# Two PSUM banks per eviction: any two banks read by one strided view, against neighbouring banks or one instruction per bank, with a new order table

## The chip, the cores and the metric

The kernel runs on one core of a Trainium2 chip. Time is device time in microseconds (us) of one execution. TensorE is called PE, VectorE DVE, ScalarE ACT, GpSimd POOL, and SP is the queue that issues DMAs. PE accumulates into PSUM, which has 8 banks of 512 float32 columns in each of the 128 partitions; here the whole of it is one tile, `ps`, and bank `u` is its columns from `512 * u`.

## The reference, cut to what matters

```python
# q, k, v: (4, 8, 768, 48); beta: (4, 8, 768)
k_n = k / (norm(k) + 1e-6)
for t in range(768):                      # a delta rule: one 48x48 state per head
    y[t] = q[t] @ state
    v_old = state^T @ k_n[t]
    state += beta[t] * outer(k_n[t], v[t] - v_old)
x = y.reshape(4, 768, 384)
h = relu(x @ w_in)                        # 384 -> 1024
u, v = h[..., :512], h[..., 512:]
v_n = (v - mean(v)) / sqrt(var(v) + 1e-6)
v_s = einsum('ts,bsd->btd', w_spatial, v_n) + b_spatial[None, :, None]
out = (u * v_s) @ w_out                   # 512 -> 384
```

## The kernel before, in words

The delta rule is done in chunks of 64 positions. The 4 x 8 heads and the 12 chunks give 24 steps (`s`), of which steps 0 to 11 are one chain through the state `st_` (tile `s`) and steps 12 to 23 another. Four steps make a group (`g`). `prep(g)` multiplies the keys of each step with themselves on PE (`kk`, 16 matmuls into two PSUM banks), copies the two banks to SBUF in one instruction (`ev`, the COPY `xt<-ps` or `wspl<-ps` of L339), and inverts small triangular blocks in a long chain of tiny operations: of groups 0 and 1 on DVE (`lanes16`, L571, L574, L576, working in a PSUM bank of its own), of groups 2 to 5 on POOL (`lanes`, L556, L561). `widen` then doubles the blocks with PE, ACT, DVE and POOL (`pi` of L641; `move`, four COPYs `xt<-xt`; `zero`, four MEMSETs of L638).

`step(s)` is the recurrence: `a_` on PE (keys times state), a subtraction on DVE (L720, `bn<-bn,ps`), `qs` and `b_` on PE, `w` on ACT (L748), `c_` on PE, the state on DVE (L761, `s<-s,ps`), `pu` on PE and the output copy `ye` on ACT (L778, `xs<-ps`). `kqt(s)` multiplies keys and queries into two banks (`kq`) and masks them on DVE (L695, `pt<-ps,mpos`). So three kinds of instruction read a pair of banks: `ev`, the mask and `ye`, 24 of each.

Every two steps yield 128 positions of two batches for the MLP: `mlp_v`, `mlp_u` (from `xh`, `xl` and `win_h`, `win_l`: each factor is split into two fp32r parts), and after each chain `gate`: the spatial product (`wsph`, `wspl` with `vf`, 792 matmuls in all) and the output product (`wout_h`, `wout_l` with `g`). The weights are split on ACT, DVE and POOL in the beginning (`win_h<-ut` of L386, `win_l` of L387). All matmuls stand under L463, since one helper issues them, and many plain copies under L339.

What runs when is written out: `P.add` records about 2,400 operations with their dependences, and `ORDER`, a table of two-letter numbers, lists them in the order in which they are issued; `PICK` says for an operation that two engines can do which one does it. Each engine works its own part of that list off in order. `Qq` in the table is a filler: one 128x256 matmul of `mpos` into a free bank (28 are built). Banks come from the pool `pm`, which is a queue: a request takes the bank that has been free longest, and an operation that wants two takes the first two, whichever they are. Banks 0 and 1 (`pc`) belong to the recurrence. An instruction that reads a pair does it through one access pattern:

```python
def banks(hs):
    a, b = sorted(h.unit for h in hs)
    v = ps[:, a * 512 : a * 512 + 256]
    return bass.AP(v.tensor, v.offset, [list(v.ap[0]), [(b - a) * 512, 2], [1, 256]])
```

The framework finds from the access patterns which instruction must wait for which, and sets semaphores. In the program as built, 38 of the reads of two banks have one to four other banks between the two (28 on ACT, 10 on DVE).

Of the kernel before, what the change touches and what calls it, by code (L numbers as in the profile page):

```python
# [17 lines left out]
GP = 4  # L18
# [24 lines left out]
    "2k4f2)2*2+2-2.5i3p3q2/2:2<5n3Z3x3c3yQq2%4N5j0[1F1f133r3s3u4g5o1G1#1T3v4h5p5l1H141s4m4O2>2?2@2[2]2^2_2{2|2}2~2,303132"
    "33342=35363738393t3A3B4Q3C4S3D4R3E4TQq4iQq4U5m5r5s5u5t1t1g4j1U1u5v4k1h4V3#3&3!3(5q8x3%3$4l3)4W5w5xQq4Z1y1z4a4d3w4c4b"
    "8l3*5y5z1vQq5!5#5$1!5%5&3F3G5(5*423+433-44454X6o1$3H3I5+5-5.5/5:5;5<5=5>6p3.463<3=3/5L4n5M1%473:3>5?5@5[5]5^5_5{5|5}"
    "5K4Y4p5N4o3?5O5P4q3;1&1(1)6g5~5,60616263643@4r4A4s4t4w4x3[1*1+8m5V8n6h4B4C4z3z5Q4u5R4D5S4(4e4&4$1-4*8o6566676n3]6i5W"
    "4E4)4y4#4%FR6j6k486l68696A6B6C6D6E6F6G5T5)6%4v5U3^498p6q6r6m8q3_4F5X6&6(4H1<5a5b4G4+6s6H6I6J6K6L6M6N6O5Z5YQq6t6u1.1/"
    "6/6x6v1:1;6y8u4!8r6!6#6z6P4-6Q6R6:1=1>6S6T6U6V6$5c5d7i6w1?6.3{1@4.6)6*4/6+5C8s8t7j4:4;8v4<5DQq6;7k8w7l6W1[6X6Y1]8!8y"
    "7(6-6Z1^6a6b6c6<6=4>4?6>3|8z7m8#6?7n1_6_6|3}6d6e7p7o6f7:8$1{4@4[4]5E6@6]4^6^8%7)5455565F7*8&575G7+6{736~716,72706}8("
    "8)8*8+8-8.8/5H587q59417-1|5I7.5J5B748:8<8=8>8?8@8[8]8^8_8{6[9n9o7s7r7t9.7u7v5A9p9q9r7w1}4=1~9s7/8|758}Qq8~8,7x7;9/7y"  # L50
    "767z7=7%7$7#7|7<4_90209192937>9:1,7!A;21777S4|4{7?7@7C7D7[7_7E947]7{229t9v95967~83817}9798997^9w239u789;7F3~9<9=A<7G"
    "7HA=9A24259B7T9x9y4}26797A7B7I9z9!A>3,4~9#808485827&86279)7,9C4,A?Ap9D879E7U7V7W9&9$7X285053292A7K9(9F9%9?9G9>9H9IQq"
    "2BA@7Z7Y8c7a7b7c9]887d898d8e9@8f7e9^2DB89[8A7f9_9{8B9J9K2C2E7J7h9|8U9L8;7LA[40512F7g9M9N9O9}8C9,A0B98D9*9+A19~A{8V8E"
    "8WAAA8A2A39-A]2GA^9P2H9Q9RA_BA2I8FA6B48G8HBB2J7M8IA}8JBCA|BDA~Qq8g8X9S9TQq7N9U8K9VBF9WQqA7A9ArA5B5BEA,7OAs8YBG8h8M7P"
    "8j8ZAq8iB2B3At8LB0Av2K9X9Y9Z9a9b9c9dBHB1BIBKBJAwBL8bAuAx7QFFFIBM8aFGABFHBRB6AyBNGPQqFJAC8N8O528PFKBO9e9f9g9h9i9j9kAz"
    "A$8QGQFOFLA4BVBQBU9lGHBPIUGYBXBY8kBTB7BWQqADAEAJAKALAMANAZAFAGAHFMGi8RA!A#A%AOAIFNAPAQAR8SA&ASATAUFPAaAbAcFQAdAeAhAi"
    "GIGJGjGKGbGcGkFVFTFSFUFWGLGMGO9mGNAjAkAlHGGdGeAmHHGRFXQqFZQqFYBZFaFbFcGfGSIIGXA(GZBSA-A)HIHJGVAgGgAfAnGWAoFdBaFeFfBb"
    "FgFiGhFjFkFlFmFnFoFpGTBxAVHKAWGUByHOBcGlHdHPGnGmGoAXFqFrFsFtFu7RGpA.HL8TA*BzBhBiBdGqFvGrHNB!BeBfBjB#GsBkBlHeHQGvILGw"
    "FwHMFxBgGtBmHkFyBnHRBoBpFzF!F#F$BqA/GxGaGyGzB(HSB)B$HTHfHgHUHhBrBsHXBtHYB*G$G!GuHZHaG#G%BuB%B&HiA+B+HlHVHWB-HnJTF%F&"
# [12 lines left out]
    "E)L)E8L-L.L(L+L<L/LlL:L;E*MbEtE+McMdMsMeMfK3MpMqE/E:E;L9LAMgE<E=E>E?E@E[MtMhE]MuMvMwMiMxL=H~MjMyE^E_LBK=K>LCH,G}E-I0"
    "K?MzM!LHK@K[LDLILJLKK^LLLMLEK_K{K|E.L>G~E{LNK4K5E|K}LFM*M-M&M)M(EuK~M+M$M%E}M.LOM/K]K,G,LGL0E~L{L|MBL}MCL?MDL@L[M@L]"
    "L^L~L,M:M;M0L1L2M<L_M1M3M2MEM=M>MFM[MGM]M^NEM_MJM4M?M{M|M5L3L4M#M}M~L5M6M,N0M7L6M8N1L7M9MKE,F0MLNFN6N7N8MMNGNHNIF7F1"
    "F2F8F9FAMNF3MOFBF4N2N3N4NMFCNNNONPN9NQNRNSNTNUL8NVNWNXNcNdNeNfNgNhNiNjNYNZO>O]F5NaNbNkNlNmN+FDMHK6N-NJNnO^NoNpNqNrN."
    "N/N:NAN;N<N=N>N?N@N[N]N^NKMQN_MAN{N|N}N~O?N,O0O1O2O3O4O5O6OSOTNBO7O8O9OAOBMPOUNsOVOWOXOYOZOaObOcOdOiOKOjOkOlOmOCOnOL"
    "OoOpOqOrOsOtOeO<N5O|OuOvOwO@NCO_O=OxO}O{N!N#ODN$NtOMN%OENuN&ONNvNwOFNxOON(OGOPF6FEO[NyNLOfOgOhO~O,P0P1P2P3P4P5P6P7P8"
    "P9PAPBPCN)N*OQNzOROyOzOHPEO!O)PFO*PGPHPIPJPKPLO+PMPDO-PNPkPlPmPOO#O.PPPnPoPQPRPpPSPTPqO/O:PrPsPtO$PuPUO%PvP!PcP#PdPV"
    "PePfPgP$P%PwPxMIOIPyOJO&O(O;PzP&Q4Q5P(Q6Q7PWPXPYPZP)P*P+P-P.P/P:P;P<P=Q8Q9QAQBQCQDPhQEQFQKQLQMQNP|QOQPQQQGQRQSP}QTQU"
    "PiNDQHQIPaPjPbQVP>P?P~P,P@P[P]Q0P^QWQXQJQYQZP_Q1QaQbQcQdQeQiQfQjQkQlQ2P{Q3QgQhQmQnQoQp"  # L80
)
PICK = (
    "11101010011110100110100000000000000000000001110011000011001100000000000000000000001100010000000000000000000000100000"
    "00000000000011000000000100000001011101000010100011000101000000000100000000001100010000001101000010000111101001000001"
    "0110011011010000110001000000"
# [3 lines left out]
class Op:  # L89
    __slots__ = ("i", "fn", "alt", "pr", "deps", "out", "acq", "rel", "give", "kind", "kb", "rate", "port", "n", "t")  # L90
# [13 lines left out]

class Plan:
# [7 lines left out]
    def add(self, eng, dur, fn, rd=(), wr=(), pr=0.0, acq=(), rel=(), give=(), port=False, kb=0, kind="", rate=190.0):  # L113
        o = Op()
        o.i, o.fn, o.pr, o.acq, o.rel, o.give, o.kind, o.kb, o.rate = len(self.ops), fn, pr, acq, rel, give, kind, kb, rate
# [30 lines left out]
    def greedy(self):  # L146
# [3 lines left out]
        refs = {}  # L150
        for o in self.ops:
# [3 lines left out]
            if not o.deps:  # L155
                ready.append(o)
        while ready:
            can = [o for o in ready if all(units[p] >= sum(q == p for q, _ in o.acq) for p, _ in o.acq)]
# [4 lines left out]
            for p, _ in o.acq:  # L163
                units[p] -= 1
            for p, h in o.rel:
                refs[h] -= 1
                units[p] += refs[h] == 0
            for p, _ in o.give:
                units[p] += 1
# [7 lines left out]
    def emit(self):  # L177

        units = {p: list(u) for p, u in self.pools.items()}
        for o in self.ops:  # L180
# [3 lines left out]
        for o, e in list(self.listed() if ORDER else self.greedy()):  # L184
            if o is None:
                if units["pm"]:
# [873 lines left out]
```

## Time and profile before

| | |
|---|---|
| median of 3 runs | 511.7 us (511.24 to 514.7) |
| profiled execution | 514.14 us, of which its span (first to last instruction) is 512.4 us |
| mean granted TensorE clock | 0.893 of full speed |
| PE busy | 444.0 us (87%) |
| DVE, ACT, POOL busy | 248.9, 248.9, 223.6 us |

The page gives the busy time of each engine, the span in 40 slices, and the chain of work that ended last, followed back from the end. A row of a group of instructions ends in the idle time of the engine just before them and what released it. A row of the timeline starts with its start and its length in us and ends, where the engine had been idle, in brackets with that idle time and the releaser. Windows give the busy time of each engine within a stretch and the clock granted to PE, 1.00 being 2.4 GHz and 0.50 being 1.2 GHz.

### The profile page before, as it was taken

How to read it: one execution, taken by the hardware profiler on the slowest of the kernel's cores; microseconds unless marked ns; L12 is line 12 of the kernel's file. 1: busy time of each engine (PE TensorE's matmuls, PEld its weight loads, DVE VectorE, ACT ScalarE, POOL GpSimd, SP SyncE). 2: the span in 40 equal slices, each digit the busy share in tenths (PEclk: the TensorE clock that was granted, in tenths of full speed). 3: DMA queues.
4: the chain of work that ended last, by engine and by line, in shares of the span. 5: the costliest groups of instructions: out<-in, count | busy, mean ns of one | idle time of the engine just before them, and what ended most of it. 6: DMA issues, size and time to landing. Idle time of an engine off the chain costs nothing.

```text
span 512.4 us, 21714 instructions
## 1 busy us (share of the span) xinstructions
PE 444.0 (87%) x9728; PEld 392.5 (77%) x9728; DVE 248.9 (49%) x543; ACT 248.9 (49%) x577; POOL 223.6 (44%) x370
## 2 busy tenths in 40 slices
PE   4547955788897998779999989999999999999997
PEld 3436743667675687567799779998898889999996
DVE  3686834742575674774652813624454123333222
ACT  1576743435486687667624622426534375323211
POOL 3024440698448980248982686480212411414000
PEclk9655556695799999998999989999999999999999
DMA  8700332024232326753204305010144000000112
GB/s 279 269 3 20 92 99 65 35 62 151 75 114 82 108 80 207 218 155 120 74 4 147 95 23 160 23 36 3 32 131 118 10 18 17 17 2 0 63 51 74
DMA packets 26109, 42.65 MB, mean 83 GB/s; under 512 B 4512, under 2 KB 14880, under 8 KB 26016
## 3 DMA queue, kind: packets, MB, share of 16 engines
q1 hardware_dynamic: 26016, 41.27, 25.5%
q8 instruction: 76, 1.25, 1.0%
q14 instruction: 17, 0.14, 0.1%
HBM read 35.36 MB, written 4.72 MB: 78 GB/s over the span
## 4 chain that ended last, share of the span: by engine, by line
PE 76%; ACT 8%; DMA 6%; DVE 5%; issue 3%; SPq 1%; ACTq 0%; DVEq 0%
PE ps L463 76%; ACT xt L339 3%; DMA bn<-in_bun 2%; DVE prod L571 1%; DVE ps L574 1%; DMA vf<-in_w_in 1%; ACT xs L778 1%; DMA ke<-in_k_t 1%; SPq L354 1%; DMA xs<-xs 1%; ACT pi L641 1%; DVE pt L695 1%; ACT w L748 1%; ACT wspl L339 0%; ACT xh L799 0%
## 5 line engine op out<-in xcount | busy, mean ns | idle before, releaser
L463 PE MATMUL ps<-wsph,vf 128*128 128x256 f32 x528 | 108.1, 286 | 1.1 <-ACT xs L778 1.1
L463 PEld LDWEIGHTS ps<-wsph,vf 128*128 128x128 f32 x528 | 86.9, 191 | 2.6 <-ACT xs L778 1.6
L561 POOL TENSOR_TENSOR wl<-wl,prod 128x60 f32<-128x60 f32 (+7 forms) x120 | 73.6, 614 | 9.3
L463 PE MATMUL ps<-wspl,vf 128*128 128x256 f32 x264 | 74.6, 282 | 0.0
L556 POOL TENSOR_TENSOR prod<-wl,la 128x60 f32<-128x60 f32 (+7 forms) x120 | 67.6, 563 | 9.3
L917 DVE TENSOR_TENSOR gt<-ps,bbc 128x512 f32<-128x512 f32 x24 | 16.6, 691 | 76.2 <-PE ps L463 64.5
L463 PEld LDWEIGHTS ps<-wspl,vf 128*128 128x128 f32 x264 | 50.4, 191 | 0.3
L463 PE MATMUL ps<-wout_h,g 128*128 128x384 f32 x128 | 35.7, 347 | 2.5 <-ACT xs L778 2.5
L339 ACT COPY xt<-ps 128x256 f32<-128x256 f32 (+1 forms) x35 | 16.5, 474 | 39.3 <-PE ps L463 39.2
L695 DVE TENSOR_TENSOR pt<-ps,mpos 128x512 f32<-128x512 f32 x24 | 16.5, 686 | 36.6 <-PE ps L463 30.6
L680 POOL TENSOR_TENSOR bn<-bn,nn 128x384 f32<-128x384 f32 x12 | 10.6, 887 | 49.1 <-DVE nn L548 24.5
L463 PE MATMUL ps<-mpos 128*128 128x256 f32 x56 | 25.7, 575 | 7.2 <-POOL mpos L378 3.0
L463 PE MATMUL ps<-ke 64*64 64x64 f32 (+2 forms) x768 | 22.0, 268 | 11.3 <-issue 4.7
L463 PEld LDWEIGHTS ps<-ke 64*64 64x64 f32 (+1 forms) x768 | 17.9, 167 | 16.1 <-issue 7.5
L339 ACT COPY xt<-xt 32x128 f32<-32x128 f32 (+1 forms) x82 | 28.7, 350 | 1.7
L463 PEld LDWEIGHTS ps<-wout_h,g 128*128 128x128 f32 x128 | 23.7, 193 | 2.9 <-ACT xs L778 2.6
L748 ACT COPY w<-ps 128x384 f32<-128x384 f32 x24 | 11.5, 478 | 28.3 <-PE ps L463 28.2
L463 PE MATMUL ps<-pt,w 64*48 64x64 f32 x768 | 18.6, 242 | 7.3 <-ACT w L748 6.0
L882 ACT ACTIVATE ut<-ps 128x256 f32<-128x256 f32 x48 | 17.3, 380 | 14.7 <-PE ps L463 14.7
L463 PE MATMUL ps<-bn 64*64 64x64 f32 (+2 forms) x896 | 20.3, 242 | 4.6 <-ACT wspl L339 2.6
L922 ACT CAST xt<-gt 128x512 fp32r<-128x512 f32 x8 | 5.0, 620 | 38.7 <-DVE gt L920 28.7
L463 PEld LDWEIGHTS ps<-pt,w 64*48 64x48 f32 x768 | 14.9, 138 | 11.1 <-ACT w L748 7.2
(209 smaller groups left out, 1085.8 us busy)
## 6 DMA issues: line engine op xcount, KB each, us to landing
bn<-in_bun SPq DMA_DIRECT2D x46, 256.0 KB, 3.5
bn<-in_bun SPq DMA_DIRECT2D x48, 192.0 KB, 3.7
ke<-in_k_t SPq DMA_DIRECT2D x22, 256.0 KB, 3.4
out<-ob SPq DMA_DIRECT2D x24, 192.0 KB, 2.0
vf<-in_w_in SPq DMA_DIRECT2D x6, 512.0 KB, 6.7
g<-in_w_sp SPq DMA_DIRECT2D x3, 768.0 KB, 6.4
g<-in_w_out SPq DMA_DIRECT2D x4, 384.0 KB, 3.6
xs<-xs SPq DMA_DIRECT2D x66, 16.0 KB, 2.6
```

What stands on the lines that cost most here:

```text
L339: (nc.scalar.copy if e == "ACT" else ENG[e].tensor_copy)(out=out_, in_=in_)
L354: return P.add("SP", 0.39 if k.get("kb") else 0.57, lambda: nc.sync.dma_start(out=out_() if callable(out_) else out_, in_=in_() if callabl ...
L463: nc.tensor.matmul(o, l, r, start=start, stop=stop)
L556: P.add("POOL", cost, lambda: nc.gpsimd.tensor_tensor(out=pt if j else dst, in0=w3[:, :n, j : j + 1].broadcast_to([128, n, m]), in1=la3[:, ...
L561: P.add("POOL", cost, lambda: nc.gpsimd.tensor_tensor(out=dst, in0=dst, in1=pt, op=ALU.add), rd=["prod"], wr=[kw], pr=p0 + 2)
L571: P.add("DVE", cost, lambda: nc.vector.tensor_tensor(out=pt(), in0=w4()[:, :, :n, j : j + 1].broadcast_to([128, 2, n, m]), in1=lj.unsqueez ...
L574: P.add("DVE", cost, lambda: nc.vector.tensor_tensor(out=dst(), in0=dst(), in1=pt(), op=ALU.subtract), rd=["prod"], wr=["wp"], pr=p0 + 2)
L680: P.add("", {"DVE": 0.56, "POOL": 0.83}, fn=lambda e: ENG[e].tensor_tensor(out=v, in0=v, in1=n.unsqueeze(3).broadcast_to([128, 2, 4, HD]), ...
L695: P.add("DVE", 0.69, lambda: nc.vector.tensor_tensor(out=pt.rearrange("p (d a c) -> p d a c", d=2, a=2), in0=banks(hs).rearrange("p d (a c ...
L748: P.add("ACT", 0.48, lambda: nc.scalar.copy(out=v3(w, 192), in_=v3(pc, 512)[:, :, 0:192]), rd=["pc"], wr=[("w", s % 2)], pr=pr)
L882: nc.scalar.activation(out=dst[:, :, o * 128 : o * 128 + 128], in_=src[:, :, j], func=AF.Relu)
L917: P.add("DVE", 0.69, lambda: nc.vector.tensor_tensor(out=gt(), in0=v3(bank(h.unit), 256), in1=bbc[0][:, th * 256 : th * 256 + 256].unsquee ...
```

## The change

Pairs of banks become a request of their own, `pm2`. A new class `Banks` gives out two neighbouring banks where two are free, and otherwise the two that have been free longest. Whoever reads a pair does it with one instruction where the banks are neighbours, and with one instruction for each bank where they are not (`pairs`). Matmuls address one bank at a time (`one`). `ORDER` and `PICK` are new from the first row to the last; some durations that the planner of that table uses are changed, which changes no instruction by itself. The core of the diff, with one row of the table for all:

```diff
 ORDER = (
-    "000A0D010G0J0]1i2O02090705060403Qq0B0E0H0K080L0C0F0^0I0N3l3m1V1I0M2Q2P152l2o2m0*2M2p2N2L2r2u1w0P0QQq0R0S0T0U0V0W0_0Y"
+    "070506040A0D000102030B0E080G090H0I0C0J0]0^0K0Y0_0L0F1V1W2O3l0N0P0Q1I1i0M2P2M2l2m3m1X0R0{0S1w1a0T0U0V0W0X1J0Z1N0}0b0c"
...
+class Banks:
+    def __init__(self, banks):
+        self.free, self.n = {b: i for i, b in enumerate(banks)}, len(banks)
+
+    def find(self, two):
+        f = self.free
+        if not two:
+            return min(f, key=f.get, default=None)
+        b = min((b for b in sorted(f) if b + 1 in f), key=lambda b: max(f[b], f[b + 1]), default=None)
+        if b is not None:
+            return b, b + 1
+        return tuple(sorted(sorted(f, key=f.get)[:2])) if len(f) > 1 else None
...
-    def banks(hs):
-
-        a, b = sorted(h.unit for h in hs)
-        v = ps[:, a * 512 : a * 512 + 256]
-        return bass.AP(v.tensor, v.offset, [list(v.ap[0]), [(b - a) * 512, 2], [1, 256]])
+    def pairs(h):
+
+        a, b = h.unit if h else (0, 1)
+        if b == a + 1:
+            yield slice(0, 2), v3(ps[:, a * 512 : a * 512 + 1024], 512)[:, :, 0:256]
+        else:
+            for d in range(2):
+                yield slice(d, d + 1), ps[:, h.unit[d] * 512 : h.unit[d] * 512 + 256].unsqueeze(1)
+
+    def one(h, d):
+        k = h.unit[d] if h else d
+        return ps[:, k * 512 : k * 512 + 256]
...
-            def ev(e, s=s, view=view):
-                copy(e, v3(xt_of(s // GP)[:, s % GP * 512 : s % GP * 512 + 512], 256), view())
+            def ev(e, s=s, h=h):
+                for d, v in pairs(h):
+                    copy(e, v3(xt_of(s // GP)[:, s % GP * 512 : s % GP * 512 + 512], 256)[:, d], v)
...
-        P.add("", {"ACT": 1.04, "POOL": 0.86}, move, rd=d, wr=o, pr=pr)
-        P.add("", {"DVE": 0.76, "POOL": 0.84}, zero, wr=d, pr=pr)
+        P.add("", {"ACT": 1.25, "POOL": 1.3}, move, rd=d, wr=o, pr=pr)
+        P.add("", {"DVE": 0.88, "POOL": 1.1}, zero, wr=d, pr=pr)
...
-                    mm(banks(hs)[p * 64 : p * 64 + 64, d, c0 : c0 + 64], ks(b, 0, d, a, p, j, 64), ks(b, 512, d, a, p, j, 64))
+                    mm(one(h, d)[p * 64 : p * 64 + 64, c0 : c0 + 64], ks(b, 0, d, a, p, j, 64), ks(b, 512, d, a, p, j, 64))
...
+        def mask():
+            for d, v in pairs(h):
+                nc.vector.tensor_tensor(
+                    out=pt.rearrange("p (d a c) -> p d a c", d=2, a=2)[:, d], in0=v.rearrange("p d (a c) -> p d a c", a=2),
+                    in1=mpos.unsqueeze(1).unsqueeze(1).broadcast_to([128, v.shape[1], 2, 128]), op=ALU.mult)
...
         def ye():
             x = xs_(xo)
-            nc.scalar.copy(
-                out=x.rearrange("p (d q t) -> p d q t", d=2, q=4)[0:KR, :, :, s % 2 * 64 : s % 2 * 64 + 64],
-                in_=banks(hs)[0:KR].rearrange("p d (q t) -> p d q t", q=4))
+            for d, v in pairs(h):
+                nc.scalar.copy(
+                    out=x.rearrange("p (d q t) -> p d q t", d=2, q=4)[0:KR, d, :, s % 2 * 64 : s % 2 * 64 + 64],
+                    in_=v[0:KR].rearrange("p d (q t) -> p d q t", q=4))
```

In the program as built, no read has another bank between its two any more. Nine pairs are read in halves: 4 of `ye` and 5 of the mask, none of `ev`. Of `move`'s copies 9 more are on ACT and 9 fewer on POOL; 2 `ev` copies go from DVE to ACT, 4 of POOL's tensor operations to DVE, and 25 fillers are built instead of 28. There are 234 DMAs as before.

Three places of the new order, in which `ps` is PSUM, `xt` and `wspl` hold the blocks of a group, and `pt` is the masked product of keys and queries. First ACT, from the last copies of group 1's products (`xt1<-ps 128x512`) to `w0` of step 2. Before:

```order
L339 COPY xt1_998<-ps_97 128x512 x2
L339 COPY xt1_998<-xt1_998 32x16x32 x4
L386 CAST win_h_61<-ut1_387 128x512
L386 CAST win_h_61<-ut2_389 128x512
L339 COPY xt0_261<-ps_97 128x4x64
L339 COPY xt0_261<-xt0_261 32x4x32 x4
L799 CAST xh_1310<-xs0_913 128x768
L748 COPY w0_75<-ps_97 128x384
```

and now:

```order
L391 COPY xt1_1006<-ps_97 128x512
L440 CAST win_h_61<-ut5_395 128x512
L391 COPY xt1_1006<-ps_97 128x512
L391 COPY xt1_1006<-xt1_1006 32x16x32
L440 CAST win_h_61<-ut3_339 128x512
L391 COPY xt1_1006<-xt1_1006 32x16x32 x2
L693 ACTIVATE pi_70<-ps_97 128x256
L855 CAST xh_1236<-xs0_987 128x768
L391 COPY xt1_1006<-xt1_1006 32x16x32
L391 COPY xt0_222<-ps_97 128x4x64
L391 COPY xt0_222<-xt0_222 32x4x32 x4
L803 COPY w0_75<-ps_97 128x384
```

The same work stands ahead of `w0`, in a finer mixture: a weight cast lies between the last two copies of `xt1`, and others have moved further ahead.

Second DVE, in the chain of group 1's inversion (`prod` and `ps` by turns; it has 30 operations), where the state of step 1 is updated (`s<-s,ps`). Before:

```order
L571 TENSOR_TENSOR prod_67<-ps_97,wspl_84 128x126
L574 TENSOR_TENSOR ps_97<-ps_97,prod_67 128x2x9x7
L548 STREAM_TRANSPOSE nn1_96<-nl_93 128x32
L571 TENSOR_TENSOR prod_67<-ps_97,wspl_84 128x120
L574 TENSOR_TENSOR ps_97<-ps_97,prod_67 128x2x10x6
L571 TENSOR_TENSOR prod_67<-ps_97,wspl_84 128x110
L574 TENSOR_TENSOR ps_97<-ps_97,prod_67 128x2x11x5
L571 TENSOR_TENSOR prod_67<-ps_97,wspl_84 128x96
L761 TENSOR_TENSOR s_77<-s_77,ps_97 112x384
```

and now:

```order
L623 TENSOR_TENSOR prod_67<-ps_97,wspl_84 128x126
L816 TENSOR_TENSOR s_77<-s_77,ps_97 112x384
L626 TENSOR_TENSOR ps_97<-ps_97,prod_67 128x2x9x7
L623 TENSOR_TENSOR prod_67<-ps_97,wspl_84 128x120
L750 TENSOR_TENSOR pt0_71<-ps_97,mpos_66 128x512
```

The update stood behind 23 instructions counted from the chain's first; now it stands behind 16.

Third ACT, at a `ye` whose banks are not neighbours. It is now, where one instruction of 112x8x64 stood before:

```order
L834 COPY xs0_3057<-ps_97 112x4x64 x2
```

The pair is read in two halves.

## Rows read from the trace of the kernel before

**Rows 1.** The page, parts 1 and 2 (40 slices of 12.8 us) and 4.

```profile
PE 444.0 (87%) x9728; PEld 392.5 (77%) x9728; DVE 248.9 (49%) x543; ACT 248.9 (49%) x577; POOL 223.6 (44%) x370
...
PE   4547955788897998779999989999999999999997
...
PEclk9655556695799999998999989999999999999999
...
PE 76%; ACT 8%; DMA 6%; DVE 5%; issue 3%; SPq 1%; ACTq 0%; DVEq 0%
```

**Rows 2.** Windows: start:end, length, busy us (instructions) by engine, PE clock, DMA.

```profile
40.00:172.00 132.00, 102.83 (x3224) 82.41 (x3228) 73.16 (x163) 69.59 (x165) 76.54 (x134) 0.71 0.27 80
200.00:300.00 100.00, 87.40 (x2210) 74.30 (x2211) 57.35 (x114) 57.53 (x135) 58.93 (x98) 0.97 0.38 118
```

**Rows 3.** Timeline of DVE, ACT and PE between 48 and 92 us.

```profile
48.72 0.58 ACT L339 COPY wspl<-ps 128x512 f32<-128x512 f32 x1 [2.91 <-PE ps L463]
...
71.94 0.20 DVE L576 SCALAR_TENSOR_TENSOR ps<-ps,wspl 128x30 f32<-128x30 f32 x1 [8.45 <-ACT xt L339]
...
71.96 1.14 PE L463 MATMUL ps<-ke 64*64 64x64 f32 x32 [1.47 <-ACT xt L339]
...
76.72 0.30 DVE L574 TENSOR_TENSOR ps<-ps,prod 128x126 f32<-128x126 f32 x1
...
78.49 0.54 DVE L761 TENSOR_TENSOR s<-s,ps 112x384 f32<-112x384 f32 x1
...
79.09 1.10 PE L463 MATMUL ps<-s,bn 48*64 48x48 f32 x32 [5.14 <-DVE s L761]
...
83.55 1.11 PE L463 MATMUL ps<-bn,s 48*48 48x64 f32 x32
...
84.72 0.59 ACT L339 COPY xt<-ps 128x512 f32<-128x512 f32 x1 [12.82 <-PE ps L463]
...
91.84 1.10 PE L463 MATMUL ps<-pt,w 64*48 64x64 f32 x32 [5.21 <-ACT w L748]
```

**Rows 4.** Timeline of PE and DVE around the mask at 107 us.

```profile
103.78 0.69 PE L463 MATMUL ps<-bn 64*64 64x64 f32 x32
...
105.65 0.68 PE L463 MATMUL ps<-s,bn 48*64 48x48 f32 x32
...
107.11 0.69 DVE L695 TENSOR_TENSOR pt<-ps,mpos 128x512 f32<-128x512 f32 x1 [4.34 <-PE ps L463]
...
108.28 0.52 DVE L720 TENSOR_TENSOR bn<-bn,ps 128x384 f32<-128x384 f32 x1
```

**Rows 5.** Timeline of PE after 134 us: five of its waits.

```profile
134.14 0.73 PE L463 MATMUL ps<-gi,bbc 16*32 16x16 f32 x60 [0.51 <-ACT xs L778]
...
163.28 0.50 PE L463 MATMUL ps<-win_h,xh 128*128 128x512 f32 x1 [1.81 <-ACT xs L778]
...
207.50 0.60 PE L463 MATMUL ps<-pt,w 64*48 64x64 f32 x27 [1.18 <-ACT xt L339]
...
298.69 0.69 PE L463 MATMUL ps<-wout_h,g 128*128 128x384 f32 x1 [2.48 <-ACT xs L778]
...
387.80 0.38 PE L463 MATMUL ps<-wsph,vf 128*128 128x256 f32 x1 [0.67 <-ACT xs L778]
```

**Rows 6.** Groups by shape: mean prices of masks, copies and moves.

```profile
L695 DVE TENSOR_TENSOR pt<-ps,mpos 128x512 f32<-128x512 f32 x24 | 16.5, 686 | 36.6 <-PE ps L463 30.6 <-ACT xs L778 4.2 <-ACT ut L882 1.5
L339 ACT COPY xt<-xt 32x128 f32<-32x128 f32 x68 | 20.1, 296 | 1.5
L778 ACT COPY xs<-ps 112x512 f32<-112x512 f32 x22 | 12.8, 581 | 20.1 <-PE ps L463 20.1
L339 ACT COPY xt<-ps 128x256 f32<-128x256 f32 x18 | 6.6, 368 | 11.3 <-PE ps L463 11.3
```

**Rows 7.** Windows of two early stretches in which PE had the full clock.

```profile
100.20:117.20 17.00, 13.92 (x578) 11.21 (x574) 7.74 (x14) 4.51 (x12) 15.20 (x24) 1.00 0.23 69
134.30:165.00 30.70, 26.25 (x914) 21.19 (x913) 21.19 (x52) 22.13 (x57) 16.09 (x32) 1.00 0.30 88
```

More of the change, by code (lines that the diff above doesn't have):

```diff
@@ L43 @@
[L43 to L47, printed above, removed]
@@ L86 @@
+    "0001000101000001101011001000"
 )
 class Op:
-    __slots__ = ("i", "fn", "alt", "pr", "deps", "out", "acq", "rel", "give", "kind", "kb", "rate", "port", "n", "t")
+    __slots__ = ("both", "i", "fn", "alt", "pr", "deps", "out", "acq", "rel", "give", "kind", "kb", "rate", "port", "n", "t")
 class Hold:
@@ L102, in get, with take, back @@
         return self.tile
+class Banks:
[9 more added lines that the diff above has]
+        return tuple(sorted(sorted(f, key=f.get)[:2])) if len(f) > 1 else None
+    def take(self, two):
+        b = self.find(two)
+        for k in b if two else (b,):
+            del self.free[k]
+        return b
+    def back(self, b, two):
+        for k in b if two else (b,):
+            self.n += 1
+            self.free[k] = self.n
 class Plan:
@@ L111, in pool, with add @@
         self.pools[name] = list(units)
-    def add(self, eng, dur, fn, rd=(), wr=(), pr=0.0, acq=(), rel=(), give=(), port=False, kb=0, kind="", rate=190.0):
+    def add(self, eng, dur, fn, rd=(), wr=(), pr=0.0, acq=(), rel=(), give=(), port=False, kb=0, kind="", rate=190.0, both=None):
         o = Op()
+        o.both = both
         o.i, o.fn, o.pr, o.acq, o.rel, o.give, o.kind, o.kb, o.rate = len(self.ops), fn, pr, acq, rel, give, kind, kb, rate
@@ L156, in greedy @@
                 ready.append(o)
+        fits = lambda p, o: banks.find(p == "pm2") is not None if p[:2] == "pm" else units[p] >= sum(q == p for q, _ in o.acq)
         while ready:
-            can = [o for o in ready if all(units[p] >= sum(q == p for q, _ in o.acq) for p, _ in o.acq)]
+            can = [o for o in ready if all(fits(p, o) for p, _ in o.acq)]
             o = min(can, key=lambda o: (max(o.t, min(free.get(e, 0.0) for e in o.alt)), o.pr, o.i))
@@ L162, in greedy @@
             free[e] = end = max(o.t, free.get(e, 0.0)) + o.alt[e]
-            for p, _ in o.acq:
-                units[p] -= 1
+            for p, h in o.acq:
+                if p[:2] == "pm":
+                    got[h] = banks.take(p == "pm2")
+                else:
+                    units[p] -= 1
             for p, h in o.rel:
                 refs[h] -= 1
-                units[p] += refs[h] == 0
-            for p, _ in o.give:
-                units[p] += 1
+                if refs[h] == 0 and p[:2] == "pm":
+                    banks.back(got[h], p == "pm2")
+                elif refs[h] == 0:
+                    units[p] += 1
+            for p, u in o.give:
+                if p == "pm":
+                    banks.back(u, False)
+                else:
+                    units[p] += 1
             for d in o.out:
@@ L185, in emit @@
             if o is None:
-                if units["pm"]:
-                    self.filler(units["pm"][0])
+                if banks.free:
+                    self.filler(banks.find(False))
                 continue
@@ L191, in emit @@
             for p, h in o.acq:
-                h.unit = units[p].pop(0)
+                h.unit = banks.take(p == "pm2") if p[:2] == "pm" else units[p].pop(0)
             if o.fn is not None:
@@ L196, in emit @@
                 h.refs -= 1
-                if h.refs == 0:
+                if h.refs == 0 and p[:2] == "pm":
+                    banks.back(h.unit, p == "pm2")
+                elif h.refs == 0:
                     units[p].append(h.unit)
             for p, u in o.give:
-                units[p].append(u)
+                if p == "pm":
+                    banks.back(u, False)
+                else:
+                    units[p].append(u)
         assert len(done) == len(self.ops)
@@ L477, in prep, with kk @@
                 ke, kk_ = kte[s % 2], ("ke", s % 2)
[L478 to L481 removed]
+            h = None if g == 0 and s4 == 1 else Hold()
+            bk, acq = ([], [("pm2", h)]) if h else (["pc"], ())
             ld(ke, k_t[s], wr=[kk_], pr=30 + s if g else -20 + s4, kb=256)
[L484 to L485 removed]
+            def kk(ke=ke, hold=h):
                 for pj in range(4):
@@ L726, in step @@
         xo = xhold[s // 2]
-        yacq = [("pm", h) for h in hs] + ([("xs", xo)] if s % 2 == 0 else [])
+        yacq = [("pm2", h)] + ([("xs", xo)] if s % 2 == 0 else [])
         if c:
```

134 lines of the change are left out of this document (66 added, 68 removed).

## The prediction, made before the changed kernel ran

> **What bounds the kernel now.** I read the page first, then windows, then the timeline where the windows show gaps. PE is busy 444.0 us of the 512.4 us span and makes 76% of the chain that ended last [rows 1]. The slices show two halves: from about the middle on PE stands at 9 tenths and at nearly the full clock, and only less matmul work could shorten that part; in the first third it stands at 4 to 8. So the time to be won is PE's idle time ahead of 300 us. The windows size it: between 40 and 172 us PE is busy 102.83 of 132 us, so 29.2 us are idle, and between 200 and 300 us 12.6 us are [rows 2].
>
> The timeline tells what ends those gaps. A read of two banks is one access pattern, and the dependences are found from access patterns; if the pattern is taken to cover all that lies between its two ends, such a read waits for whoever works in a bank between them, and whoever writes there next waits for it. The rows look like that. At 84.72 ACT copies one of the two-bank products of keys (here banks 5 and 7) after 12.82 us of idling [rows 3]. The product's own matmuls began at 71.96 and took 1.14, so they had ended at 73.10. What ended just before the copy is the group of matmuls at 83.55 (1.11 long, to 84.66): `qs` of step 2, which writes bank 6. 84.66 - 73.10 = **11.6 us** of false waiting. At 71.94 DVE's inversion of group 1, which works in bank 3, waited 8.45 us for an ACT copy that reads banks 2 and 6. Behind that inversion, on the same engine, stands the state update at 78.49, for which PE waits 5.14 us at 79.09; `qs` follows it, and that releases the copy at 84.72. One false wait feeds the next, and PE waits 5.21 us again at 91.84 for `w`, which is behind that copy on ACT.
>
> **The change part by part.** None of the 38 wide reads is left, so every wait of that kind goes. I price them where they end a path.
>
> (a) The copy at 48.72 (banks 3 and 6, waiting for a matmul in bank 4) idled 2.91 us [rows 3]. ACT is the engine that feeds the first inversions there: 2.9 us.
>
> (b) and (c), the 8.45 and the 11.6 us. If (b) goes, the inversion and the state update come 8.45 us earlier, and `qs` with them, but the copy at 84.72 would then still wait. If (c) goes, ACT goes on at 73.1, whenever `qs` comes. The two stretches lie side by side in time (63.5 to 71.9 on DVE; 73.1 to 84.7 on ACT, which holds DVE's delay in it), and I count the longer, **11.6 us**. What is late next is `w`, by its own matmuls.
>
> (d) The mask at 107.11 reads banks 2 and 4, and matmuls that ended only just before it work in bank 3. Its own ended at 103.78 + 0.69 = 104.47, so 2.6 of its 4.34 us are false. The subtraction at 108.28 is queued behind it; its input, of the matmuls at 105.65 (0.68 long), was there at 106.33, and it could begin no more than 108.28 - 106.33 = 1.95 us earlier: **1.9 us** [rows 4]. The sum of the front is 2.9 + 11.6 + 1.9 = 16.4.
>
> (e) From 134 us on the work is PE's own, so only what PE itself waits counts. Eight of its waits are ended by an ACT or DVE read of a pair with PE's bank in between; five stand in [rows 5], from 0.51 at 134.14 to 0.67 at 387.80, 2.48 the longest. The five make 6.65 us and the eight together **9.1 us**. These matmuls needed no more than a bank nobody reads.
>
> The fillers fall from 28 to 25 matmuls; they fill time in which PE has nothing else, and I count them at nothing. So are the order of the DMAs (234 as before; a load of the output weights goes ahead of one of keys that is used some 40 us later) and the four tensor operations from POOL to DVE, which stand beside a busy POOL.
>
> (f) The new order. It puts the state update of step 1 ahead of seven more operations of the inversion; of before these begin at 76.72 and the update at 78.49 [rows 3], so 1.8 us at this place. Elsewhere it mixes weight casts, moves and copies differently, and no row of before shows that. The bounds: nothing below (I see no place where it moves PE work behind something later), and above, all of PE's idle time of the two windows that (a) to (e) leave. That is 29.2 - 16.4 - 4.0 = 8.8 and 12.6 - 4.4 = 8.2, where 4.0 and 4.4 are the parts of the 9.1 us that lie in the windows; together 17.0. I take half, **8.5**: the one place that can be read gives a fifth of the first window's rest, and there are several such steps.
>
> (g) Costs. A split `ye` is two copies of about the size of the 128x256 copy, 2 x 368 - 581 = 155 ns more than one; for the mask half of 512 columns I scale 686 ns (512 columns) and 544 ns (the state update, 0.54 with 384) to about 0.40 us, so 0.12 more. 4 x 0.155 + 5 x 0.12 = 1.2 us. Nine moves of 296 ns come to ACT, 2.7 us [rows 6]. Both stand beside PE's work and can cost nothing; ACT is on the path in the front, so I charge them in full: **3.9 us**.
>
> Sum: -16.4 - 9.1 - 8.5 + 3.9 = -30.1 us. The profiled execution took 514.14 us, 2.4 more than the median of 511.7, so the sum gives 484.0 on its basis and 481.6 against the median, which I forecast: **482 us**.
>
> **The rivals.**
>
> R1, only PE's own waits count. The front could be bound by the length of its recurrence and of POOL's inversions, and the copies' waits be slack that other work fills. For it speaks that PE itself is busy 78% of the first window; against it that PE's long waits there (5.14 and 5.21) hang on the delayed DVE and ACT. It would save 9.1 + 1.47 (the PE wait at 71.96) - 3.9 = 6.7: 505 us.
>
> R2, the front's stalls add up. If DVE's 8.45 us end ahead of the place where ACT's 11.6 begin, and both lie on one path, the front gives 2.9 + 8.45 + 11.6 + 2.6 = 25.6 in place of 16.4, and the sum is -25.6 - 9.1 - 8.5 + 3.9 = -39.3: 472 us. For it speaks the chain from the inversion over the state update to `qs`; against it that `qs`, pulled forward, shortens (c) by itself.
>
> R3, nothing is won. The waits might come from the banks being taken again, not from the pattern: neighbours are wanted in pairs, so a free single bank may wait for its neighbour. Then the wait of 12.82 us comes back at another bank; the sum is about zero, 512 us. Against it: at 84.72 the copy's own banks were long done. The Trainium skill's "PSUM — Partial Sum Buffer", section "PSUM bank collisions raise a hardware error", asks for guarding a read against a writer in the same bank and quadrant; by it no guard is due for bank 6, and the 11.6 us are not the chip's demand.
>
> R4, slower by the clock. PE ran at the full 2.4 GHz for 100.2 to 117.2 us and 134.3 to 165 us, busy 13.92 and 26.25 us [rows 7], between slices at 5 to 7 tenths [rows 1], where it had been idle a quarter of the time or more. If the new order spreads the same matmuls thinner there and the clock stays at 1.2 GHz, that work takes twice as long: +40.2, so -30.1 + 40.2 = +10.1, **522 us**. It decides the sign once more than about 30 us of busy time fall to the lower clock. The first third, however, gets denser when waits go, which speaks against it. "TensorE: Matmul & The Clock Gate" of the Trainium skill, section "A second HAM failure mode: psum-queue depth-cycling", tells of a kernel whose cycling through PSUM banks left PE small gaps between groups, and the clock went to and fro; by it shorter waits for banks should help, and a pool that hands out other banks could hurt. The trace agrees so far that the lower clock stands in the slices with gaps.
>
> **How the numbers follow.** Chances: forecast 0.57, R1 0.15, R2 0.19, R3 0.05, R4 0.04. The forecast's own ends: without (f) 490, with (f) whole and (g) free 469. R2 with a small (f) lies in the same stretch, and R1 with some of (f) reaches below 500. I give **468 to 500**, which leaves out R3, R4, about half of R1 and the lower part of R2, about 2 in 10. Under 1% (5 us) is what a measurement of this kernel can't tell from no change. Faster by more: forecast, R2 and R1, 0.91; within: R3, 0.05; slower: R4, 0.04.
>
> **What would show it.** Right: no ACT or DVE read of a pair waits longer than its own matmuls; the state updates and `w` of the first four steps come 12 us or more earlier by 110 us; PE has no waits on `xs` copies after 134 us; PE busy stays near 440 us, with idle time of under 15 us from 40 to 172 us of the work. (f) is right if what is left of PE's idle time in the front is clearly less than 13 us, and its lower bound is right if PE's front idle merely falls by 16. R1: the copies come early, but PE idles as before for the recurrence. R2: steps 2 to 4 come 20 us or more earlier. R3: waits of 5 to 12 us on ACT or DVE whose releasers are other engines' reads of the same banks. R4: PEclk at 5 or 6 in slices that stand at 9 now, with PE busy over 460 us. What I can't see is a wait in the new order for an operation that lies late on another engine; one of 10 us in the front would undo a third of the gain.

## The result and the profile after

The changed kernel took 486.7 us (median of 4 runs, 483.4 to 490.6) against 512.75 of before over four runs (511.7 over the three shown ahead): a ratio of 0.949, interval 0.939 to 0.960. Forecast were 482 us, 468 to 500. Intervals leave out single runs that took over 1.5% longer than the fastest of their kernel; medians keep them. The size came out; how it is made up did not, as the profile shows at once. The page after, parts 1, 2 and 4 (a slice is 12.0 us now), beside [rows 1]:

```profile
PE 426.6 (89%) x9722; PEld 380.7 (79%) x9722; DVE 247.9 (51%) x550; ACT 253.1 (53%) x592; POOL 216.4 (45%) x357
...
PE   2437888777989899998999999999899999999996
...
PEclk9555579885999999999999999999999999999999
...
PE 78%; DVE 6%; issue 6%; ACT 6%; DMA 3%; SPq 1%; DVEq 0%; ACTq 0%
```

The span fell from 512.4 to 481.7 us, by 30.7. Only 13.3 of that is PE's idle time (68.4 to 55.1); 17.4 is PE's *busy* time (444.0 to 426.6). The prediction's sum held idle time alone, and expected busy time to stay near 440. PEclk tells where that comes from: the clock stays up from the eleventh slice on, at 120 us, where before it was low up to the eighth and again in slices 10 and 11, to 141 us. The windows, beside [rows 2]:

```profile
40.00:172.00 132.00, 113.37 (x3727) 91.85 (x3723) 87.86 (x193) 81.46 (x198) 90.40 (x151) 0.84 0.35 105
200.00:300.00 100.00, 94.57 (x2224) 85.22 (x2223) 51.85 (x98) 50.68 (x121) 69.84 (x115) 1.00 0.27 81
```

PE now idles 18.6 us in the first (29.2 before) and 5.4 in the second (12.6), and the clock of the first rose from 0.71 to 0.84. The timeline after, which answers to [rows 3]: the operation of DVE that stood at 71.94, the state updates of steps 1 and 4, and `w` of step 2:

```profile
57.81 0.16 DVE L628 SCALAR_TENSOR_TENSOR ps<-ps,wspl 128x30 f32<-128x30 f32 x1
...
62.45 0.54 DVE L816 TENSOR_TENSOR s<-s,ps 112x384 f32<-112x384 f32 x1
...
69.25 0.48 ACT L803 COPY w<-ps 128x384 f32<-128x384 f32 x1
...
106.58 0.56 DVE L816 TENSOR_TENSOR s<-s,ps 112x384 f32<-112x384 f32 x1 [1.82 <-PE ps L517]
```

The wait of 8.45 us is gone, the update of step 1 comes 16.0 us earlier than at 78.49, and `w` 22.1 earlier than at 91.32 (its PE reader stood at 91.84). The update of step 4 had been at 135.62 and is 29.0 us earlier; the updates of steps 2 and 3 come 27.7 and 26.2 us earlier. That is the sign set for the rival R2 (20 us or more for steps 2 to 4). The lead does not last: the update of step 5, at 131.59 against 151.72, is 20.1 us earlier. The waits of PE by releaser (total, times, longest; `xs` copies are `ye`), of before and of after:

```profile
PE ps L463 <- issue: 13.4, 11, 4.0
PE ps L463 <- ACT xs L778: 9.8, 10, 2.5
```

```profile
PE ps L517 <- issue: 22.1, 17, 4.8
...
PE ps L517 <- ACT xs L834: 0.5, 2, 0.3
```

What [rows 5] showed is all but gone: for `ye` 9.8 us became 0.5. But idle time with no releaser grew from 13.4 to 22.1 us. The halves cost what the sum said, by shape: 149 ns more for a mask (2 x 417 - 685) and 158 for a `ye`:

```profile
L834 ACT COPY xs<-ps 112x512 f32<-112x512 f32 x18 | 10.5, 582 | 13.0 <-PE ps L517 13.0
L834 ACT COPY xs<-ps 112x256 f32<-112x256 f32 x8 | 2.6, 370 | 1.0 <-PE ps L517 1.0
```

```profile
L750 DVE TENSOR_TENSOR pt<-ps,mpos 128x512 f32<-128x512 f32 x19 | 12.9, 685 | 21.2 <-PE ps L517 21.1
L750 DVE TENSOR_TENSOR pt<-ps,mpos 128x256 f32<-128x256 f32 x10 | 3.8, 417 | 7.5 <-PE ps L517 3.9 <-ACT w L803 3.7
```

### The profile page after: what moved, and what is told of

Read it like the earlier page. It is cut to its first block, busy times and chain, and to the rows that moved or that the text cites. A ratio compares the mean times of both kernels' runs of the same rounds, so it can differ in the third digit from the quotient of the medians.

```text
span 481.7 us, 21693 instructions
## 1 busy us (share of the span) xinstructions
PE 426.6 (89%) x9722; PEld 380.7 (79%) x9722; DVE 247.9 (51%) x550; ACT 253.1 (53%) x592; POOL 216.4 (45%) x357
## 4 chain that ended last, share of the span: by engine, by line
PE 78%; DVE 6%; issue 6%; ACT 6%; DMA 3%; SPq 1%; DVEq 0%; ACTq 0%
PE ps L517 78%; DMA ke<-in_k_t 2%; ACT xt L391 1%; DVE ps L626 1%; DVE prod L623 1%; SPq L410 1%; DMA bn<-in_bun 1%; ACT gt L890 1%; DVE pt L750 1%; ACT w L803 0%; ACT ut L453 0%; ACT ut L454 0%; ACT ut L452 0%; DVE wspl L587 0%; ACT vr L880 0%
## 5 line engine op out<-in xcount | busy, mean ns | idle before, releaser
L994 ACT COPY ob<-ps 128x384 f32<-128x384 f32 x24 | 11.2, 479 | 42.6 <-PE ps L517 40.6
L391 ACT COPY xt<-xt 32x128 f32<-32x128 f32 (+1 forms) x91 | 31.7, 349 | 2.1
L391 ACT COPY xt<-ps 128x512 f32<-128x512 f32 (+1 forms) x37 | 17.7, 481 | 27.6 <-PE ps L517 27.6
L750 DVE TENSOR_TENSOR pt<-ps,mpos 128x512 f32<-128x512 f32 (+1 forms) x29 | 16.7, 593 | 28.7 <-PE ps L517 25.0
L517 PEld LDWEIGHTS ps<-bn 64*64 64x64 f32 (+1 forms) x896 | 16.9, 145 | 15.3 <-issue 4.6
L517 PE MATMUL ps<-ke 64*64 64x64 f32 (+2 forms) x768 | 18.9, 257 | 9.0 <-issue 4.8
L517 PEld LDWEIGHTS ps<-ke 64*64 64x64 f32 (+1 forms) x768 | 16.0, 160 | 13.4 <-issue 7.6
L803 ACT COPY w<-ps 128x384 f32<-128x384 f32 x24 | 11.5, 477 | 27.0 <-PE ps L517 26.9
L732 POOL TENSOR_TENSOR bn<-bn,nn 128x384 f32<-128x384 f32 x11 | 9.1, 835 | 36.4 <-DVE nn L600 15.9
L938 ACT ACTIVATE ut<-ps 128x256 f32<-128x256 f32 x48 | 17.9, 383 | 12.5 <-PE ps L517 12.4
L517 PE MATMUL ps<-wout_l,g 128*128 128x384 f32 x64 | 21.1, 337 | 0.0
L517 PE MATMUL ps<-s,bn 48*64 48x48 f32 x704 | 16.4, 231 | 4.9 <-issue 3.5
```

The costliest lines, as they stand in the source:

```text
L391: (nc.scalar.copy if e == "ACT" else ENG[e].tensor_copy)(out=out_, in_=in_)
L517: nc.tensor.matmul(o, l, r, start=start, stop=stop)
L732: P.add("", {"DVE": 0.56, "POOL": 0.83}, fn=lambda e: ENG[e].tensor_tensor(out=v, in0=v, in1=n.unsqueeze(3).broadcast_to([128, 2, 4, HD]), ...
L750: nc.vector.tensor_tensor(out=pt.rearrange("p (d a c) -> p d a c", d=2, a=2)[:, d], in0=v.rearrange("p d (a c) -> p d a c", a=2), in1=mpos ...
L803: P.add("ACT", 0.48, lambda: nc.scalar.copy(out=v3(w, 192), in_=v3(pc, 512)[:, :, 0:192]), rd=["pc"], wr=[("w", s % 2)], pr=pr)
L938: nc.scalar.activation(out=dst[:, :, o * 128 : o * 128 + 128], in_=src[:, :, j], func=AF.Relu)
```

## The experiments

The change has two parts that can be had apart: how pairs are taken and read, and the order table. "Idle" is the profiled span less PE's busy time, of one execution. Each ratio is to runs of the kernel before beside the kernel's own; their medians go from 511.05 to 514.33.

| kernel | reads of pairs | order | median us | ratio to before (95%) | PE busy / idle us |
|---|---|---|---|---|---|
| before | any two, one wide read | old | 511.7 | 1 | 444.0 / 68.4 |
| changed | neighbours or halves | new | 486.7 | 0.939 to 0.960 | 426.6 / 55.1 |
| new banks, old order | neighbours or halves | old | 483.5 | 0.944 to 0.948 | 434.7 / 45.0 |
| old banks, new order | any two, one wide read | new | 515.5 | 1.005 to 1.013 | 441.7 / 76.0 |
| halves, old order | any two, halves | old | 479.2 | 0.932 to 0.941 | 432.6 / 46.3 |
| halves, new order | any two, halves | new | 486.5 | 0.937 to 0.952 | 427.5 / 57.7 |
| four halves in the front | any two, four split | old | 505.2 | 0.985 to 0.992 | 444.2 / 58.8 |
| (c) alone | any two, one split | old | 507.0 | 0.987 to 0.994 | 438.1 / 64.2 |
| front alone | any two, front split | old | 493.8 | 0.946 to 0.967 | 434.1 / 58.0 |
| late alone | any two, rest split | old | 498.2 | 0.959 to 0.973 | 439.7 / 58.5 |

**The reads without the order.** The edit replaces the tables in the changed kernel.

```diff
-ORDER, PICK = (the new tables)
+ORDER, PICK = (the tables of the kernel before)
```

> The changed kernel's bank pool and reads, with the order table and the choices of engine of the kernel before. Theory A (false waits cost what the prediction's terms (a) to (e) say, 25.5 us, less about 1 us for splits; the new order the rest): 486 to 491 us, PE's idle time falls by 20 us or more and its busy time stays near 440. Theory B (the new order does most of it): 500 us or more. Theory C (the gain comes in good part as TensorE's clock: waits go, PE gets denser, the clock rises earlier): PE's busy time falls too, by 8 us or more, in the stretch from 60 to 140 us.

483.5 us, below the 486 to 491 of theory A. The idle time fell by 23.4 us, as A says, and the busy time by 9.3, as C says; that it fell in the stretch which C names was not read. B, that the order does most of it, is out. Nearly all pairs are still read in one instruction here (8 of 72 are not), so it is not the halves as such that win.

**The order without the reads.**

```diff
-ORDER, PICK = (the tables of the kernel before)
+ORDER, PICK = (the new tables)
```

> The kernel before with the new order table and choices of engine alone: pairs are any two banks, read by one strided view. Theory A: the order is worth some 8 us and meets false waits of its own (about as many wide reads as before), so 500 to 512 us. Theory B: 495 us or less. If the order was made for the new pool and hurts with the old one, 515 us or more.

515.5 us, slower than before by 0.5% to 1.3%: the last of the three cases. Under the old reads the order is worth nothing, and less. Waits of PE in it:

```profile
PE ps L463 <- DVE pt L695: 7.8, 10, 1.4
PE ps L463 <- ACT xt L339: 7.6, 6, 3.3
PE ps L463 <- ACT xs L778: 5.9, 10, 0.7
```

PE waits 21.3 us for masks and copies. In the program as built, 47 reads have other banks between their two, against 38 before, so this pair does not price the order by itself.

**The false waits and nothing else.** In the kernel before, each pair that is not of neighbours is read in two instructions; banks, order and engines stay.

```diff
-    copy(e, dst, view())
+    for d, v in pairs(hs, ("ev", s)):   # both banks at once if |a - b| == 1,
+        copy(e, dst[:, d], v)           # else one instruction for each bank
...                                      (mask and ye alike)
```

> The kernel before, same pool and same order, but every pair that is not of neighbours is read in two instructions (38 of 72). It takes the false waits away and moves nothing. Theory A: 486 to 493 us, up to 5 us above the kernel with the new pool and the old order, since 38 splits at 0.12 to 0.16 us each are 5 us if all lie on the path. If the pool's neighbours matter by themselves: 8 us or more above it.

479.2 us, the best so far and below the 486 to 493 of theory A, although it has 38 splits where the changed kernel has nine. Together with the kernel above, which took the same waits away with few splits, that is the proof that the waits were false: nothing was moved, and 32.5 us went. Its rows, for the copy of 84.72 and the `w` behind it, are

```profile
68.45 0.65 ACT L351 COPY xt<-ps 128x256 f32<-128x256 f32 x2 [0.21 <-PE ps L475]
...
75.11 0.47 ACT L764 COPY w<-ps 128x384 f32<-128x384 f32 x1
```

16.3 and 16.2 us earlier. The pool that prefers neighbours is not needed, and is behind halves of any two banks by 4.3 us in the old order (the intervals, 0.944 to 0.948 and 0.932 to 0.941, do not meet) and by nothing in the new one.

**Four splits of the front**, those of the terms (a) to (d).

```diff
+SPLIT = {("ev", 6), ("ev", 11), ("ev", 10), ("mask", 3)}   # all others stay wide
```

> The kernel before with only four reads in halves: those of the prediction's terms (a) at 48.72, (b) the copy that DVE's inversion waited for at 71.94, (c) at 84.72 and (d) at 107.11 us. Theory A: 16.4 us less, 494 to 498 us. If the front's stalls add up in series (the rival R2): 25 us less, 486 to 488. If other wide reads of the front take over the waits: 503 us or more.

505.2 us: 6.5 us, not 16.4, the last case. `w` of step 2 came at 81.03 and the update of step 4 at 124.83, each over 10 us earlier, but other wide reads took waits over, and PE's own waits for `ye` stayed.

**One split**, the copy of 84.72 us.

```diff
+SPLIT = {("ev", 10)}
```

> The kernel before with one read in halves: term (c), the copy at 84.72 us, whose false part was 11.6 us. The prediction counted (b) and (c) side by side as 11.6, of which (c) alone would give 11.6 and (b) alone nothing. If that holds: the copy goes out some 11 us earlier, the w of step 2 (91.32) too, and 500 us or a little more, if nothing behind gives it back. From the four splits, which moved w of step 2 by 10.3 us and gave 6.5 us at the end: w earlier by 2 to 10 us and 505 to 509. If (b) holds (c) back (the copy's own banks come late as long as the inversion does): w earlier by under 3 us and no measurable gain.

507.0 us, 4.1 below its own before (511.05). The middle case: `w` came at 82.55, 8.8 us earlier. The rows say why not more:

```profile
75.17 0.68 DVE L710 TENSOR_TENSOR pt<-ps,mpos 128x512 f32<-128x512 f32 x1
```

```profile
75.89 0.65 ACT L351 COPY xt<-ps 128x256 f32<-128x256 f32 x2 [8.75 <-DVE pt L710]
```

The copy in halves still idles 8.75 us, now for the mask of step 2, which reads banks 2 and 6 by one wide pattern and so covers banks 3 to 5 as well, one of the copy's own among them. Both only read; they are kept apart all the same. Behind the false wait stood a second one, on another engine. The wait of before does not name it, since it ended earlier, but the timeline of before has this mask too:

```profile
79.93 0.68 DVE L695 TENSOR_TENSOR pt<-ps,mpos 128x512 f32<-128x512 f32 x1
```

It ended at 80.61, 7.5 us behind the copy's own matmuls (73.10) and 4.1 ahead of the copy.

**Front and late apart.**

```diff
+SPLIT = {ev of steps 0 to 11, ye of 0 to 3, mask of 0 to 4}      # front alone
+SPLIT = {all others}                                             # late alone
```

> The kernel before with the reads in halves for the front alone: the copies of groups 0 to 2, the masks of steps 0 to 4, the output copies of steps 0 to 3 (21 pair reads, those that are not neighbours split). Four splits of the front gave 6.5 us where the prediction's terms (a) to (d) said 16.4. If the other wide reads of the front took the waits over: 20 us or more less than before, 485 to 492 us, and the state update of step 4 at about 117 us as in the kernel with all reads split. If what the front wins is given back later whatever is split there: 500 us or more, with that update at about 117 us all the same.

> The complement: all other pair reads in halves, from step 4 on, the front as in the kernel before. By the prediction's term (e) 9.1 us less, 502 to 504 us. If front and late add up, this and the front-only kernel together give the 32.5 us of all splits. If the late waits only matter once the front is fast, 508 us or more; if they cost more than PE's own waits show, 497 or less.

493.8 and 498.2 us, 20.6 and 16.1 less than before beside them (514.3). The first meets "20 us or more less" but not 485 to 492; the second is under the 502 to 504 that term (e) gave. In the profiled spans the front gives 20.3 us (10.4 of idle, 9.9 of busy time), the late part 14.2 (9.9 and 4.3), and all splits 33.5: the two add up. With the front's other reads split as well, the copy of term (c) waits for nothing worth naming:

```profile
69.09 1.20 ACT L351 COPY xt<-ps 128x256 f32<-128x256 f32 x4 [0.62 <-PE ps L475]
```

**The new order with halves**, and two hybrids of the orders that ask where it loses.

```diff
-ORDER, PICK = (old tables)
+ORDER, PICK = (new tables)                                       # halves, new order
+ORDER = new[:512] + (what is left, in the old order)             # new front
+ORDER = old[:193] + (what is left, in the new order)             # old start
```

> The new order table with the old pool and all pairs that are not neighbours read in halves. If the pool of neighbours is what costs the new kernel some us against old order with splits (483.5 against 479.2 with the old order): about 482 us, 4 to 5 below the changed kernel. If the new order by itself is worse by a few us with any pool: 482 to 486, above the same reads in the old order (479.2). Theory A's term (f), 8.5 us won by the order, would give 471.

> Old pool and all splits; the new order up to the state update of step 4 (its first 512 entries), then what is left in the old order. In the new order that update came at 106.6 us against 117 with the old order, yet the end came no earlier. If the new order loses what it won behind step 4: 470 to 475 us, faster than both orders. If the front's lead is worth nothing since PE's own work bounds all that follows: 478 to 482. If the new front itself is what costs (its PE idles 5 us more in the first 30 us): 482 or more.

> Old pool, all splits, the old order up to the first state copy (its first 193 entries), then what is left in the new order. The mirror of the last hybrid, which had the new front and the old rest (482.3). Old order with all splits took 479.2, new order with all splits 486.5. If the new order loses in its start (PE idles 5 us more in its first 30 us): 479 to 483. If it loses later, where PE idles near 105 and from 200 us on: 485 or more.

486.5 us, where term (f) asked for 471; 482.3 with the new front and the old rest; 486.8 with the old start and the new rest. The old order's 479.2 has other runs of before beside it (511.7) than these (514.3 and, for the last, 511.05), so the ratios to before decide: 0.932 to 0.941 for the old order, 0.937 to 0.952 for the new, 0.928 to 0.942 for the new front, and 0.947 to 0.956 for the new rest. The new front costs nothing that can be told and wins nothing. What costs, as far as these splices tell, is the new rest, whose interval does not meet the old order's (486.8 is 24.3 us under its own before, 479.2 is 32.5 under its own). The new front has 21 fillers and the new rest 31, in place of 28. In the changed kernel the lead is lost within one step: with the new banks the update of step 4 is at 106.58 in the new order and at 117.11 in the old, that of step 5 at 131.59 and 133.07. The chain of waits of the changed kernel (start, length, what) holds between them 19.36 us of PE's own work:

```profile
112.83 19.36 PE ps L517 x392
```

The new order needs 25.0 us from one update to the next (106.58 to 131.59), the old one 16.0 with the same banks. PE was busy 20.88 us of the 25.0 and 15.77 of the 16.0. In the old order all of it ran at the upper level of the clock (1.00); in the new one a part did not:

```profile
110.00:120.00 10.00, 8.65 (x245) 6.41 (x249) 4.39 (x16) 6.83 (x18) 2.53 (x8) 0.52 0.02 5
```

**Fillers.** Old order, halves, without the 28 fillers, and without the first seven alone.

```diff
-    self.filler(units["pm"][0])     # never, or not in the first 150 entries
```

> Old order, old pool and all splits, without the 28 filler matmuls, which took 22.7 us of PE there (fillers left out change no output). Of PE's time that is not the matmuls of the task, 69.0 us in that kernel, the fillers are a third. If they only fill time in which PE has nothing else: the same time, 477 to 482. If they hold the clock up: the matmuls of the task take longer than 409.9 us, and 485 us or more. If some stand ahead of work: 470 to 476.

477.1 us (0.926 to 0.940): no difference from 479.2 that can be told, the first case. PE's busy time fell by 14.4 us and its idle time rose by 8.6.

> Old order, old pool and all splits, with the first 7 fillers left out (those of the first 30 us) and the other 21 or so kept. With all 28 the full clock of the start ended at 25 us and the kernel took 479.2 us; without any it ended at 70 us and the kernel took 477.1. If the early fillers end the full clock of the start: full clock until 50 us or later and 470 to 477 us. If the clock falls at 10 to 26 us all the same, as in the kernel before and the changed one, and no filler matters: 477 to 482. If the later fillers were the harmful ones: 479 or more.

482.9 us (0.934 to 0.946), which settles nothing: its six runs, spread from 475.7 to 484.8, cover all three cases. Its profile reads full clock until 90 us, which the last section takes up.

## Why the prediction was right, and where not

**That the waits are false**, and go with the pattern: shown, by the kernel that splits and moves nothing, and by the one that takes neighbours in the old order. R3 is out. The Trainium skill's "PSUM — Partial Sum Buffer", section "PSUM bank collisions raise a hardware error", asks for a guard by bank and quadrant; the runs agree that nothing more is due. R1 (505) is out too: the delays of DVE and ACT were on the path, and the front's splits alone gave 493.8.

**Terms (a) to (d), 16.4 us.** The term held idle time alone. All reads of the front together gave 10.4 us of idle time, a third less, and 9.9 of busy time, which no term held; that 20.3 is near the term is luck in part. As four prices it was wrong: the four gave 6.5 us, and (c) alone 4.1 where it was priced at 11.6. The step that failed took for each wait the releaser that came last, and the end of the input's own matmuls (73.10) as the next bound. The mask of step 2, at 79.93 in the trace of before, stood between, and had to be split as well. The worth of a false wait is read only when all reads of the kind around it are gone.

**(b) and (c) side by side.** With all reads split, `w` of step 2 came 16.2 us earlier, where (a) and the longer of (b) and (c) make 14.5 and R2's serial count 22.9. Side by side is the nearer. The 22.1 us of the changed kernel, which look like R2, hold 4.6 us of the new order: with the same banks and the old order `w` stood at 73.86. R2's sign thus came (updates 26 to 29 us earlier), but with the new order's help: with all reads split in the old order, the updates of steps 2 to 4 come 18.0 to 18.9 us earlier.

**(e), 9.1 us.** Late splits alone took 9.9 us of idle time, which hits the term (PE's waits for `ye` fell from 9.8 to 1.8), and another 4.3 us of PE's busy time.

**(f), 8.5 us for the new order: wrong.** In all three pairs with equal reads the new order is not faster: 515.5 against 511.7, 486.7 against 483.5, 486.5 against 479.2. By the ratios it loses 0.9%, 0.3% and 0.8%, about 2 to 5 us. Only in the first pair, which has more false waits, is a loss clear of the noise; in the other two the intervals overlap. I took half of PE's remaining idle time from one place where DVE's queue was better; that lead is real (10.5 us at step 4), but it is spent by step 5, on more of PE's own work and in part at the lower clock. The mark set for it, PE's idle time in the front clearly under 13 us, was missed with 18.6, and the lower bound, a fall by 16, too (10.6); so was the general mark of under 15. In the old order the same window idles 11.5 us with the new banks and 13.8 with halves. So of the 10.1 us that PE idles more in the new order (55.1 against 45.0 with the same banks), 7.1 lie in this window and 3.0 ahead of it. What in the order makes them is not settled; the idle time without a releaser is 22.1 us there and 10.4 in the old order.

**(g), 3.9 us of costs.** The prices per split were right (149 and 158 ns for 120 and 155), but they cannot all be on the path: the kernel with 38 splits is the fastest of those with all fillers. The Trainium skill's "VectorE: DVE Perf Modes", section "The TRN2 errata — SBUF-src ops pay a fixed extra latency per instruction", gives a fixed 120 cycles at 0.96 GHz for a PSUM read on VectorE and 172 at 1.2 GHz on ScalarE; 125 and 143 ns by that, an estimate, against 149 and 158 measured. The fillers, counted at nothing, are worth nothing that can be told: without all 28 the time was the same.

**The term that was missing is the clock.** 444.0 us of busy time became 432.6 with halves in the old order, with the same 9,728 matmul records, and 426.6 in the changed kernel, where the fillers' own rows fell from 25.7 to 18.3 us:

```profile
L463 PE MATMUL ps<-mpos 128*128 128x256 f32 x56 | 25.7, 575 | 7.2 <-POOL mpos L378 3.0 <-ACT xs L778 2.3 <-ACT wsph L799 1.5
```

```profile
L517 PE MATMUL ps<-mpos 128*128 128x256 f32 x50 | 18.3, 465 | 0.0
```

In the stretch from 40 to 172 us PE stands denser (113.37 us busy of 132 against 102.83) and more of it is at the upper of the clock's two levels (2.4 GHz, the other being 1.2): R4 with its sign turned round. The traces bear it out. PE's busy time at the lower level, the first microseconds counted as the last section has them, was 84.3 us before, 59.5 with halves in the old order, 66.5 with new banks in the old order, and 52.0 in the changed kernel. Half of what left the lower level is 12.4, 8.9 and 16.2 us, an estimate that lets busy time halve at the upper level; the busy time fell by 11.4, 9.3 and 17.4.

So the sum that the runs show is 25.5 us of waits, which measured 22 to 23 of idle time in the old order, plus 9 to 11 us of busy time, less about 2 to 5 us for the order. The share of the clock is read from this account; no run changed the clock alone. The forecast of 482 was near by luck: an order worth 8.5 us stood in for a clock worth about as much.

## What to carry to other kernels

An access pattern that jumps over a resource can be tracked as if it held all that lies between; splitting such a read costs some 150 ns, and a wait that it takes away can cost 10 us. Do not price such waits one by one from their last releaser: behind one stands the next, so remove all of a kind at once and then look. Look beside PE's idle time at what its busy time may do: here it moved by 9 to 17 us. And measure a new order apart from the change that it comes with.

## What the runs showed of the hardware

The profile's clock reads full from the start until the trace's first record of it, and that reading does not hold. Two windows (columns as in [rows 2]) and three rows of the kernel with halves and all fillers:

```profile
0.00:20.00 20.00, 8.96 (x356) 7.49 (x357) 8.95 (x17) 3.36 (x6) 4.54 (x22) 1.00 0.87 305
40.00:60.00 20.00, 18.01 (x615) 14.35 (x619) 16.74 (x29) 15.16 (x36) 10.91 (x18) 0.50 0.22 57
```

```profile
2.96 1.22 PE L475 MATMUL ps<-mpos 128*128 128x256 f32 x2 [2.96 <-POOL mpos L390]
...
49.52 1.22 PE L475 MATMUL ps<-mpos 128*128 128x256 f32 x2
...
73.39 0.70 PE L475 MATMUL ps<-mpos 128*128 128x256 f32 x2
```

Two matmuls of a filler take 1.22 us in the first window, as at 49.52, where the clock reads 0.50; at 73.39, where it reads 1.00, they take 0.70. So PE began at the lower level. The kernel without fillers reads full clock for 70 us:

```profile
40.00:60.00 20.00, 15.71 (x603) 13.89 (x605) 17.06 (x33) 17.25 (x43) 10.93 (x16) 1.00 0.38 114
```

Yet 32 matmuls `ps<-pt,w` take 1.10 us at 48.23 there, as long as at 52.95 in the kernel with fillers (1.10, at 0.50), and 0.66 at 85.78. With the seven first fillers left out, two matmuls of a filler take 1.22 us at 46.84, in a window that reads 1.00, and 0.70 at 67.89. So leaving fillers out did not keep the clock up: with the stretch ahead of the first record counted at the lower level, PE was busy 60.6 us at that level without fillers and 59.5 with them. The mean granted clocks of these kernels count that stretch as full and are too high, each by another amount (the first record stands at 22 us with the fillers and at 63 without); they should not be compared. Two runs of the changed kernel, at mean clocks of 0.925 and 0.974, took 483.41 and 483.45 us, and the two at 0.913 and 0.916 took 489.99 and 490.64; what the last two lost is not shown.
